# Retention and SwiGLU on one core: the chain of chunk states reads its pairs from PSUM

## The chip, the cores and the metric

The kernel runs on one core of a Trainium2 chip. The metric is the time of one execution on the device in microseconds. The engines work on their own instruction streams and are ordered by semaphores: TensorE (PE in the profile) multiplies matrices into PSUM, VectorE (DVE), ScalarE (ACT) and GpSimd (POOL) do elementwise work, and SyncE (SP) issues transfers.

## The reference

Two blocks follow each other. The first is a retention layer without softmax, on 8 batches, 8 heads, 576 positions and 64 values per head:

```python
scores = scale * np.matmul(q, k.transpose(0, 1, 3, 2))
Dmat = np.where(rel >= 0, gamma[:, None, None] ** rel[None, :, :], 0.0)   # rel = row - column
ret = scores * Dmat[None, :, :, :]
return np.matmul(ret, v)
```

Its output, with the heads laid side by side, is a matrix of 4608 tokens by 512. The second block is a SwiGLU feed-forward layer on it:

```python
g = x @ w_gate                       # 512 -> 1536
silu = g * (1.0 / (1.0 + np.exp(-g)))
return (silu * (x @ w_val)) @ w_out  # 1536 -> 512
```

All of it is fp32.

## The kernel before

**Retention.** Since the decay is a power of the distance, a head's 576 positions are cut into 9 chunks of 64. Within a chunk the scores are computed, masked with the decay and multiplied by v. What earlier chunks contribute comes through a state of 64 x 64 values for each chunk, which is the last state times a decay plus the chunk's own product of keys and values. Two heads are worked on at once, one on each half of the 128 partitions. That makes 4 head pairs per batch (`HP`) and 32 in all, numbered `i` from 0.

The products of keys and values of 8 chunks are made by `new_states` (L542) in `z`, which is half of a PSUM tile of two banks called `inner`: `z[:, 0]` has the even chunks, in one bank, and `z[:, 1]` the odd ones, in the other, 4 chunks of 64 columns each. The other halves of the two banks hold the scores, `sc` (L572). From `z` the states are made in four steps, in the function `masked`:

- `copies` (L583): ScalarE copies `z[:, 0]` to `even` in SBUF.
- `pairs` (L593): VectorE makes, for each pair of chunks, decay x `even` + `z[:, 1]`, and writes the 4 results into the odd places of `state` in SBUF.
- `odd` (L598): three VectorE instructions of 64 columns run along the chain of pairs: each is two chunks' decay times the last odd state plus the pair's own value, in place.
- `evens` (L603): one VectorE instruction makes the other states out of the odd ones and `even`.

Beside them, `own` (L579) masks the scores and `last` (L588) those of the ninth chunk. `earlier_values` (L558) multiplies the finished states with the queries in PSUM's tile `outer`, one tick later, and `to_x` writes the result into the feed-forward input.

**Feed-forward.** The first 512 tokens are done plainly: `up0` (L761, L766) and `down0` (L773). The other 4096 go in four tiles of 1024 tokens, with a fast scheme of 26 products per 4 x 4 x 4 block product: `up_step` (L992) and `down_step` (L1039) each multiply one combination of operands into one of four PSUM banks, `bankA` to `bankE`, in turn; `reads` (L926, L929, L1013, L1016, L1019) has ScalarE, VectorE and GpSimd combine the banks' contents with partial sums in SBUF. The sums of operands (`add`, L795, and L963) are made by VectorE and GpSimd as they come up.

**Order.** The order on each engine is the order in which the kernel is written out (a manual schedule). A `tick(t)` sends TensorE the products of head pair `t-1` and the values of `t-2`; what VectorE and ScalarE have to do for them is cut in pieces. The first four pairs, `i < HP`, are done at the start. Pairs 4 to 11 come while the first tokens pass `up0` and `down0`, with all pieces at once. From pair 12 on the ticks are spread among the steps of the first and later tiles, and `part_on` and `go_on` put one piece, or one part of one, behind the next step; `pairs`, `odd` and `evens` are three such parts. Before the next tick sends TensorE its products, all remaining pieces are written out.

Each engine takes its instructions strictly in order, so a bank read (L929) that stands behind a part of the state update waits for it, and so does the next matmul into that bank. `z` is one buffer: the next pair's `new_states` waits until it has been read.

Of the kernel before, what the change touches and what calls it, by code (L numbers as in the profile page):

```python
# [17 lines left out]
ALU = mybir.AluOpType  # L18
# [136 lines left out]
def kernel(  # L155
# [32 lines left out]
    nc = tc.nc  # L188
# [5 lines left out]
    HP = H // 2  # L194
    L = D
    NC = S // L
    NFULL = S // P
# [29 lines left out]
    z = inner[:, :, 256:512].rearrange("p r (c d) -> p r c d", d=D)  # L227
# [21 lines left out]
    at = [4096 + 512 * i for i in range(4)] + [x0_at + 512 * i for i in range(4)]  # L249
# [84 lines left out]
    step = tab[:, 2 * H : 2 * H + 2 * HP]  # L334
# [96 lines left out]
    even = const.tile([P, NFULL, D], F32, name="even")  # L431
# [8 lines left out]
    def places(i):  # L440
        return other if i < HP and i % 2 else (ret, ret_last, state)

    def last_scores(i):
        return bankE[:, 0:L] if i < HP else sr
# [10 lines left out]
    def vector(i):  # L455

        return i == 0
# [117 lines left out]
    def masked(i):  # L575
        p, sr, (ret, ret_last, state) = i % HP, last_scores(i), places(i)

        def own():
            nc.vector.tensor_tensor(out=ret, in0=sc, in1=near[:, 2 * p : 2 * p + 2].unsqueeze(2).to_broadcast([P, 2, NFULL, L]),  # L579
                                    op=ALU.mult)  # L580

        def copies():
            (nc.vector.tensor_copy if vector(i + 1) else nc.scalar.copy)(out=even, in_=z[:, 0])  # L583

        odd_states = state[:, 1:].rearrange("p (c r) d -> p c r d", r=2)[:, :, 1]

        def last():
            nc.vector.tensor_tensor(out=ret_last, in0=sr, in1=last_near[:, p], op=ALU.mult)  # L588

        def pairs():  # L590

            at = odd_states
            nc.vector.scalar_tensor_tensor(out=at, in0=even, scalar=step[:, p : p + 1], in1=z[:, 1], op0=ALU.mult, op1=ALU.add)  # L593

        def odd():
            at = odd_states
            for c in range(1, NFULL):
                nc.vector.scalar_tensor_tensor(out=at[:, c], in0=at[:, c - 1], scalar=step[:, HP + p : HP + p + 1],  # L598
                                               in1=at[:, c], op0=ALU.mult, op1=ALU.add)

        def evens():
            at = state[:, 0 : NC - 1].rearrange("p (c r) d -> p c r d", r=2)
            nc.vector.scalar_tensor_tensor(out=at[:, :, 1], in0=at[:, :, 0], scalar=step[:, p : p + 1], in1=even,  # L603
                                           op0=ALU.mult, op1=ALU.add)

        return [copies, own, [last, pairs, odd, evens]]

    def to_x(i):
# [66 lines left out]
    def tick(t, lo=HP, hi=NP, spread=False, then=None):  # L675
        go_on(len(pieces))
        if hi == HP:

            if lo <= t - 1 < hi:
                scores(t - 1, True)  # L680
                new_states(t - 1)
                pieces.extend(masked(t - 1))
                go_on(3)
            if lo <= t - 2 < hi:
                own_values(t - 2)
            for f in transposes(t) if lo <= t < hi else ():
                f()
            if t + 1 == HP:
                split(0)
            if lo <= t - 2 < hi:  # L690
                earlier_values(t - 2)
                if t == HP:
                    rounding(2)
                    rounding(3)
                to_x(t - 2)[0]()
            if t + 1 == HP:
                rounding(0)
            return
# [8 lines left out]
        if lo <= t - 1 < hi and whole(t - 2) and not whole(t - 1):  # L707
            decay(slice(0, H), slice(0, H), half[1])
        copies, *masks = masked(t - 1) if lo <= t - 1 < hi else (lambda: None,)
        keys, *new = transposes(t) if lo <= t < hi else (lambda: None,)  # L710
        outputs = to_x(t - 2)[0] if lo <= t - 2 < hi else lambda: None
# [96 lines left out]
    for line in OUT_SUMS:  # L808
        i, s = line.split("|")
# [395 lines left out]
```

## Time and profile before

| | us |
|---|---|
| median of three runs | 1046.8 |
| lowest and highest run | 1046.59 and 1056.34 |
| the profiled execution's own time | 1047.18 |
| its span, first to last instruction | 1045.5 |
| TensorE busy | 1027.6 |
| VectorE busy | 653.9 |
| GpSimd busy | 401.9 |
| ScalarE busy | 297.2 |

In lines of the profile, `128x64 f32<-128x64 f32 x90` means 128 partitions of 64 elements written and read, 90 instructions. Behind the bar of a group stand its busy time in us and the mean of one in ns, then the engine's idle time just before them with what ended it. A line of the timeline has start and duration in us. `x3` there is three instructions in a row, shown as one. TensorE's granted clock is at full speed (0.998).

### The profile page before, as it was taken

The numbers are of one execution on the slowest core, as the hardware profiler recorded it, in microseconds if no ns is written. First come the engines' busy times: TensorE is split into PE (matmuls) and PEld (weight loads), VectorE is DVE, ScalarE is ACT, GpSimd is POOL, SyncE is SP. The second block draws the span as 40 slices with busy tenths as digits, with TensorE's granted clock in tenths as the row PEclk, the third lists the DMA queues.
The fourth block names the chain that finished last, engine by engine and source line by source line (L and its number), as shares of the span: only waits on it lengthen the run. The fifth ranks groups of instructions, "written<-read, shape, count | busy, mean of one in ns | idle before, by whom it ended". The sixth has DMA issues, their size and how long they took to land.

```text
span 1045.5 us, 21496 instructions
## 1 busy us (share of the span) xinstructions
PE 1027.6 (98%) x8448; PEld 843.9 (81%) x8448; DVE 653.9 (63%) x1063; ACT 297.2 (28%) x646; POOL 401.9 (38%) x347
## 2 busy tenths in 40 slices
PE   7999999999999999999999999999999999999998
PEld 6444555888888888888888888888888888888887
DVE  4678878777769757555357786535476644344644
ACT  3466423243533222232322102223120022231110
POOL 2002367767476035612223048312250483222505
PEclk9999999999999999999999999999999999999999
DMA  9999867776678887665676777545554565555653
GB/s 248 242 283 258 198 197 267 207 212 182 186 204 227 239 249 200 193 178 149 176 220 159 214 182 220 154 136 155 154 174 140 153 200 152 152 153 161 181 161 101
DMA packets 310380, 199.10 MB, mean 190 GB/s; under 512 B 220168, under 2 KB 254984, under 8 KB 310280
## 3 DMA queue, kind: packets, MB, share of 16 engines
q1 hardware_dynamic: 279000, 161.51, 57.2%
q10 hardware_dynamic: 31280, 36.22, 10.4%
q8 instruction: 67, 1.10, 0.5%
q14 instruction: 33, 0.27, 0.1%
HBM read 157.56 MB, written 40.11 MB: 189 GB/s over the span
## 4 chain that ended last, share of the span: by engine, by line
PE 76%; DVE 4%; DMA 1%; ACT 0%; issue 0%; POOL 0%; ACTq 0%; DVEq 0%
PE bankC L992 12%; PE bankE L992 12%; PE bankA L992 11%; PE bankB L992 11%; PE bankA L1039 6%; PE bankB L1039 6%; PE bankC L1039 6%; PE bankE L1039 6%; DVE rest L929 1%; PE outer L531 1%; PE inner L572 1%; DVE state L598 1%; PE outer L558 1%; PE inner L542 1%; DVE arena L1016 1%
## 5 line engine op out<-in xcount | busy, mean ns | idle before, releaser
L929 POOL TENSOR_TENSOR rest<-rest 128x512 f32<-128x512 f32 x65 | 92.1, 1421 | 296.7 <-DVE rest L929 277.9
L1013 ACT ACTIVATE io<-rest 128x256 f32<-128x256 f32 x180 | 74.9, 416 | 305.3 <-DVE rest L929 259.1
L992 PE MATMUL bankA<-rest,arena 128*128 128x256 f32 x544 | 128.9, 380 | 1.8 <-DVE rest L929 1.0
L992 PE MATMUL bankC<-rest,arena 128*128 128x256 f32 x544 | 129.2, 380 | 1.4 <-DVE rest L929 1.4
L795 POOL TENSOR_TENSOR arena<-arena 128x512 f32<-128x512 f32 (+1 forms) x72 | 112.5, 1574 | 38.3 <-DMA up<-arena 22.4
L992 PE MATMUL bankE<-rest,arena 128*128 128x256 f32 x512 | 121.4, 380 | 1.0 <-DVE rest L929 1.0
L992 PE MATMUL bankB<-rest,arena 128*128 128x256 f32 x512 | 121.2, 379 | 0.0
L992 PEld LDWEIGHTS bankA<-rest,arena 128*128 128x128 f32 x544 | 103.0, 190 | 16.9 <-issue 1.9
L1020 POOL TENSOR_TENSOR arena<-rest,io 128x256 f32<-128x256 f32 x72 | 52.1, 729 | 167.3 <-ACT io L1013 167.3
L992 PEld LDWEIGHTS bankC<-rest,arena 128*128 128x128 f32 x544 | 102.8, 190 | 16.3 <-issue 1.8
L992 PEld LDWEIGHTS bankE<-rest,arena 128*128 128x128 f32 x512 | 97.0, 190 | 14.7 <-DVE rest L929 1.4
L992 PEld LDWEIGHTS bankB<-rest,arena 128*128 128x128 f32 x512 | 97.0, 190 | 13.4 <-issue 0.2
L795 POOL TENSOR_TENSOR rest<-rest 128x256 f32<-128x256 f32 (+1 forms) x66 | 67.8, 1048 | 100.9 <-DVE rest L419 61.2
L929 DVE TENSOR_TENSOR rest<-bankB,rest 128x512 f32<-128x512 f32 x72 | 48.8, 686 | 65.6 <-PE bankB L992 49.7
L929 DVE TENSOR_TENSOR rest<-bankC,rest 128x512 f32<-128x512 f32 x72 | 48.9, 687 | 64.6 <-PE bankC L992 45.9
L929 DVE TENSOR_TENSOR rest<-bankA,rest 128x512 f32<-128x512 f32 x72 | 48.8, 685 | 61.1 <-PE bankA L992 43.5
L929 DVE TENSOR_TENSOR rest<-bankE,rest 128x512 f32<-128x512 f32 x71 | 48.2, 687 | 60.5 <-PE bankE L992 46.1
L1016 DVE SCALAR_TENSOR_TENSOR arena<-rest,io 128x256 f32<-128x256 f32 x84 | 57.8, 689 | 11.1 <-ACT io L1013 10.9
L1039 PE MATMUL bankC<-arena 128*128 128x256 f32 x252 | 58.4, 381 | 0.3 <-issue 0.3
L1039 PE MATMUL bankB<-arena 128*128 128x256 f32 x252 | 58.3, 381 | 0.0
L1039 PE MATMUL bankA<-arena 128*128 128x256 f32 x252 | 58.0, 380 | 0.2 <-DVE arena L795 0.2
L1039 PE MATMUL bankE<-arena 128*128 128x256 f32 x252 | 57.9, 379 | 0.0
(189 smaller groups left out, 1632.4 us busy)
## 6 DMA issues: line engine op xcount, KB each, us to landing
arena<-up SPq DMA_DIRECT2D x234, 256.0 KB, 2.7
arena<-dn SPq DMA_DIRECT2D x104, 384.0 KB, 3.9
up<-arena ACTq DMA_DIRECT2D x78, 256.0 KB, 4.1
dn<-rest SPq DMA_DIRECT2D x78, 128.0 KB, 1.9
out_dram<-rest SPq DMA_DIRECT2D x31, 256.0 KB, 3.7
qk<-in_q_dram SPq DMA_DIRECT2D x108, 72.0 KB, 2.4
qk<-in_k_dram SPq DMA_DIRECT2D x108, 72.0 KB, 3.1
rest<-in_moe_w_out_dram ACTq DMA_DIRECT2D x6, 1024.0 KB, 5.4
```

The costliest lines, as they stand in the source:

```text
L531: m = nc.tensor.matmul(value(i, hl, c), s["v"][rows, at], ret[rows, c % 2 if whole(i) else hl, c // 2], start=start, stop=start, skip_grou ...
L542: nc.tensor.matmul(z[half[hl], r, c], s["kn"][chunk(i, hl, 2 * c + r, i < HP)], s["v"][rows, at], start=True, stop=True, skip_group_check= ...
L558: nc.tensor.matmul(xr[half[hl]] if c + 1 == NC else value(i, hl, c), state[half[hl], c, :], s["qT"][half[hl], column(i, hl, c)], start=Fal ...
L572: nc.tensor.matmul(sc[chunk(i, hl, 2 * c + r)[0], r if whole(i) else hl, c], kT[half[hl], at], qT[half[hl], at], start=True, stop=True, sk ...
L598: nc.vector.scalar_tensor_tensor(out=at[:, c], in0=at[:, c - 1], scalar=step[:, HP + p : HP + p + 1], in1=at[:, c], op0=ALU.mult, op1=ALU.add)
L795: eng.tensor_tensor(out=dst, in0=srcs[0], in1=srcs[1], op=ALU.add if op[0] == "add" else ALU.subtract)
L929: eng.tensor_tensor(out=at(op[1]), in0=at(op[2]), in1=at(op[3]), op=ALU.add if op[0] == "add" else ALU.subtract)
L992: m = nc.tensor.matmul(b[:, gv * TB : (gv + 1) * TB], w[:, gv, ts(c, P)], rhs[:, c, :], start=(opens and gv == 0 and c == 0), stop=(c == 1 ...
L1013: nc.scalar.activation(out=s, in_=src[:, 0:TB], func=AF.Silu, scale=-1.0 if negative else 1.0)
L1016: return lambda: nc.vector.scalar_tensor_tensor(out=dst, in0=src[:, TB : 2 * TB], scalar=-1.0, in1=s, op0=ALU.mult, op1=ALU.mult)
L1020: nc.gpsimd.tensor_tensor(out=dst, in0=src[:, TB : 2 * TB], in1=s, op=ALU.mult)
L1039: nc.tensor.matmul(b[:, m * TB : (m + 1) * TB], lhs[:, qd, ts(m, P)], w[:, qd], start=(opens and qd == 0 and m == 0), stop=(qd == NQ - 1), ...
```

## The change

For pairs from 4 on (`i >= HP`), only the first of the four pair states is written to `state`. The other three are written back to the place in `z[:, 1]` that they were read from, in PSUM. The chain, `odd`, then takes its second input from there, and `evens` takes the even chunks' products from `z[:, 0]` in place of the copy `even`. The copy is still made, since `pairs` reads it. For the first four pairs all is as before.

```diff
         odd_states = state[:, 1:].rearrange("p (c r) d -> p c r d", r=2)[:, :, 1]
+        firsts, summed = (NFULL, odd_states) if i < HP else (1, z[:, 1])
...
         def pairs():

-            at = odd_states
-            nc.vector.scalar_tensor_tensor(out=at, in0=even, scalar=step[:, p : p + 1], in1=z[:, 1], op0=ALU.mult, op1=ALU.add)
+            for at, c in ((odd_states[:, :firsts], slice(0, firsts)), (summed[:, firsts:], slice(firsts, NFULL))):
+                if firsts < NFULL or c.start == 0:
+                    nc.vector.scalar_tensor_tensor(out=at, in0=even[:, c], scalar=step[:, p : p + 1], in1=z[:, 1, c],
+                                                   op0=ALU.mult, op1=ALU.add)

         def odd():
             at = odd_states
             for c in range(1, NFULL):
                 nc.vector.scalar_tensor_tensor(out=at[:, c], in0=at[:, c - 1], scalar=step[:, HP + p : HP + p + 1],
-                                               in1=at[:, c], op0=ALU.mult, op1=ALU.add)
+                                               in1=summed[:, c], op0=ALU.mult, op1=ALU.add)

         def evens():
             at = state[:, 0 : NC - 1].rearrange("p (c r) d -> p c r d", r=2)
-            nc.vector.scalar_tensor_tensor(out=at[:, :, 1], in0=at[:, :, 0], scalar=step[:, p : p + 1], in1=even,
+            nc.vector.scalar_tensor_tensor(out=at[:, :, 1], in0=at[:, :, 0], scalar=step[:, p : p + 1], in1=even if i < HP else z[:, 0],
                                            op0=ALU.mult, op1=ALU.add)
```

## The prediction

> **What bounds the kernel now.** I read the page first, then TensorE's gaps, then the VectorE rows the change touches, then the two places where they meet.
>
> ```profile
> span 1045.5 us, 21496 instructions
> PE 1027.6 (98%) x8448; PEld 843.9 (81%) x8448; DVE 653.9 (63%) x1063; ACT 297.2 (28%) x646; POOL 401.9 (38%) x347
> ```
>
> TensorE is busy for all but 17.9 us of the span. About 8 us of that lie at the start and the end. So no edit to VectorE can give more than what is left in TensorE's gaps, and the question is which gaps these instructions cause. The waits of TensorE, longest first, name them:
>
> ```profile
> PE bankA L471 <- DMA qk<-in_q_dram: 4.3, 1, 4.3
> PE bankC L476 <- issue: 1.7, 1, 1.7
> PE bankC L992 <- DVE rest L929: 1.4, 1, 1.4
> PE bankA L992 <- DVE rest L929: 1.0, 1, 1.0
> PE bankE L992 <- DVE rest L929: 1.0, 1, 1.0
> PE bankA L992 <- ACT rest L926: 0.7, 1, 0.7
> PE outer L566 <- DVE kT L489: 0.5, 1, 0.5
> ```
>
> The columns are: total us, times, longest. Three waits for a bank that VectorE has still to read out (L929) make 3.4 us. Next the groups of VectorE, shapes kept apart (busy us, mean ns):
>
> ```profile
> L598 DVE SCALAR_TENSOR_TENSOR state<-state,tab 128x64 f32<-128x64 f32 x90 | 43.3, 481 | 2.9
> L603 DVE SCALAR_TENSOR_TENSOR state<-state,tab,even 128x256 f32<-128x256 f32 x30 | 14.3, 477 | 0.0
> L593 DVE SCALAR_TENSOR_TENSOR state<-even,tab,inner 128x256 f32<-128x256 f32 x30 | 14.1, 471 | 0.0
> ...
> L588 DVE TENSOR_TENSOR ret_last<-outer,last_near 128x64 f32<-128x64 f32 x28 | 6.0, 214 | 0.0
> ```
>
> L598, the chain of states, has a mean of 481 ns, while the answer on that line gives 271/285/1853 ns as least, median and most. A quarter of the length of L593's operands can't cost more than L593 does: the excess over 285 ns is a stall inside the instruction. Summed over all 96 of them it is 17.7 us, and only 0.1 us of it lies in the first four head pairs, which the change leaves alone. L593, which takes one input from PSUM, never exceeds 472 ns. The timeline shows where a stalled L598 meets a gap of TensorE (start, duration; the bracket is idle time before):
>
> ```profile
> 318.45 0.68 DVE L929 TENSOR_TENSOR rest<-bankB,rest 128x512 f32<-128x512 f32 x1
> 319.05 3.29 DVE L598 SCALAR_TENSOR_TENSOR state<-state,tab 128x64 f32<-128x64 f32 x3
> 322.27 1.28 DVE L929 TENSOR_TENSOR rest<-bankC,rest 128x512 f32<-128x512 f32 x2
> ...
> 319.23 1.27 POOL L963 TENSOR_TENSOR arena<-arena 128x512 f32<-128x512 f32 x1
> 320.45 1.81 POOL L795 TENSOR_TENSOR arena<-arena 128x768 f32<-128x768 f32 x1
> ...
> 323.69 1.97 PE L992 MATMUL bankC<-rest,arena 128*128 128x256 f32 x8 [1.44 <-DVE rest L929]
> ```
>
> Three chain steps take 3.29 us instead of 0.93 (3 x 285 and two gaps of 36 ns), and end with the GpSimd instruction beside them, at 322.26. The bank reads queued behind them end at 323.5, and TensorE starts late by 1.44 us. The same at 265 to 269 us: three steps take 2.75 us beside GpSimd additions, two reads of bankA follow to 268.9, and bankA's next matmul has waited 1.04 us.
>
> **What the Trainium skill says.** "SBUF — State Buffer", section "Who interferes with whom": "A DVE instruction with two SBUF inputs contends with a GpSimd instruction that reads SBUF"; the later one waits for the whole of the other. The trace agrees: L598 has two SBUF inputs and reaches 1853 ns beside GpSimd, L593 with one stays at 472. "VectorE: DVE Perf Modes", section on the TRN2 errata, prices a PSUM source at 120 cycles plus the elements against 58 for SBUF at 0.96 GHz, so 65 ns more. The trace disagrees: 256 elements take 471 ns with a PSUM input (L593) and 479 without (L603). I keep 65 ns as an upper bound for the forms not shown here. "PSUM — Partial Sum Buffer", on bank collisions, says that software must keep two engines off one bank; so the bank of z stays closed to TensorE until VectorE's last read of it.
>
> **The change part by part.** It acts in 28 of the 32 head pairs.
>
> Pairs (L593). One instruction of 256 elements becomes two, 64 elements to SBUF and 192 to PSUM. The slope comes from two rows: 64 elements take 214 ns (L588), 512 take 691 (median of L579), so 1.065 ns per element. Then 64 cost 471 - 192 x 1.065 = 267 ns, and 192 cost 471 - 64 x 1.065 = 403 ns, plus a gap of 36: together 706 instead of 471. No row shows VectorE writing PSUM. Below, there is no reason that it beats an SBUF write by more than the 14 ns between L598's least and median; above, 65 ns. I take 0.
>
> Chain (L598). Three steps read one input from PSUM: 267 instead of 285 ns, and no second SBUF input, so the stalls go. Gain 54 ns, and the 17.6 us.
>
> Even states (L603). In1 comes from PSUM: 471 instead of 479 ns.
>
> Sum without stalls, from start to end of a head pair's states: now 1.83 us (471 + 3 x 285 + 479, three gaps of 36, an overlap of 83); after, 2.00. So VectorE does 0.17 us more, 4.8 us over 28, against 17.6 us of stalls: 12.8 us net of its 654. If each of the six PSUM forms cost 65 ns more, it is 0.56 us each, 15.7 us in all.
>
> What of it lies on the path. At 322 us: the reads of bankC would run at 320.2 to 321.4, TensorE is ready at 322.25; the gap of 1.44 goes, with 0.8 us to spare. At 268 us: the reads of bankA end at 267.3 and TensorE is ready at 268.0; 1.04 goes, with 0.7 to spare. The 0.51 us before L566 at 274.9 waits for the key transposition (L489), at the end of a run of VectorE and ScalarE work that started behind the same stall: ScalarE's two SiLUs, its scalings of k and q and then the transposes move up by about 1.6 us, TensorE by 1.04; 0.51 fits. Sum 2.99 us. The third wait (bankE, 1.0 us at 192.8) ends a VectorE-bound run from 164 us on; pair 11 (counted from 0) at that run's head carries only 0.11 us of stall, against 0.17 more work: plus 0.06.
>
> Where do the other stalls go? 17.6 minus those at the two places (1.8 and 2.4) were hidden: VectorE idles after them, waiting for TensorE. What is late next after 323 us is VectorE's sums for the down projection; VectorE moves up by 2.2 us there and TensorE by 1.44, so the 0.2 us wait at 361 doesn't grow.
>
> Added waits. The even states now read z, so TensorE's next new_states (L542) waits for them, and not for the pairs alone. Behind L542 stand that tick's matmuls and all feed-forward steps. From the end of L603 to the next L542 there are at least 3.19 us (near 120 to 139 us, and more later): 0.17, or 0.56, is covered. Before L558, which reads the states, the least is 0.76 us, at pair 11: 0.06 is covered there too. ScalarE's copy of z[:, 0] into `even` need wait only for the pairs: no gain, since it comes 5.4 us or more after L603. The pairs' second half waits for its first, counted. No DMA moves, and SP's queue stays as it is. A few instructions of ScalarE and one sum of GpSimd name a DMA semaphore that another wait had implied until now. ScalarE's are loads ordered two head pairs ahead; the GpSimd sum, at 329.6 us, waits 7.4 us for VectorE anyway. I cost them at nothing.
>
> **Sum.** 1047.18 - 2.99 + 0.06 = 1044.25 against the profiled execution's own time; the median of the runs is 0.38 below that: 1043.9 us.
>
> **The rivals.**
> - Hidden anyway, or the lock moves on. VectorE's next instruction with two SBUF inputs meets the GpSimd work that L598 met. For: L1016 (two SBUF inputs) shows 1.24 us beside GpSimd for a row of 0.42. Against: at both places the next in line reads a bank, with one SBUF input. If it comes behind the bank reads, the transposition's 0.51 and one of the two gaps (1.44) stay: 1043.9 + 1.95 = 1045.8; with all of it kept, 1046.8.
> - Slower. The longer state update delays the bank reads queued behind it where no stall is removed. It pays per head pair what TensorE can't wait: 0.17 us, 0.56 with the skill's price. It decides where a bank read has less slack than that. Now TensorE waits for L929 in three places only, so few can be that close; were all 28 exposed at 0.17, it costs 4.8 and the sum is 1043.9 + 4.8 = 1048.7; at 0.56, 1059.6. Slower than before needs 18 exposed pairs at 0.17, or 6 at 0.56.
> - The change does not do what it says: PSUM operands don't spare the lock. L593's 472 ns at most speaks against it. It would end at 1046.8 plus part of the 0.17s, 1047.5.
>
> **How the numbers follow.** Forecast 1043.9 (1043 to 1045): 0.52. Lock moves or hidden (1045 to 1047.2): 0.28. No sparing: 0.05. Slower (from 1047.2, mostly to 1049): 0.11. Another 0.04 for a gain over 4 us, if GpSimd runs freer as well. Leaving out what is above 1047.5 and below 1042.8 gives the range. A difference of 1% is 10.5 us, about what a measurement of this kernel can tell from no change; only slower at the skill's price with nearly all pairs exposed reaches it (0.04), and no gain does, as TensorE's gaps hold too little (0.01).
>
> **What would show it.** L598's mean falls to about 270 ns with no long ones, its input named inner; L593 splits into some 267 and 403; VectorE's busy time falls to about 641 us, or stays above 648 where the lock moves on to L1016 or L1019; TensorE's waits for L929 on bankC (1.4) and bankA (1.0) are gone. I would be wrong if the 192-element form took far over 470 ns, if L542 waited for VectorE, or if new waits for L929 appeared at other ticks.

## The result, and the profile after

The changed kernel takes 1043.78 us (median of 20 runs), against 1047.6 for the kernel before (20 runs). The ratio is 0.9959, with a 95% interval of 0.9944 to 0.9973: between 2.8 and 5.9 us off, or 4.3. The profiled execution has a time of its own of 1045.08 us, 2.1 below that of before. Single runs of one kernel lie up to 4.4 us below their median and up to 8.7 above it, so one time tells little here, and the experiments go by intervals and by where TensorE waits. (The two medians lie 3.8 us apart; the ratio is the better guide.)

Line numbers move by up to three: L593 has become L595, L598 is L601, L603 is L606, L929 is L932, L992 is L995 and L1039 is L1042. The page of after:

```profile
span 1043.4 us, 21528 instructions
...
PE 1026.9 (98%) x8448; PEld 842.8 (81%) x8448; DVE 641.2 (61%) x1091; ACT 296.8 (28%) x646; POOL 400.4 (38%) x347
```

VectorE lost 12.7 us of busy time with 28 instructions more. Its groups for the states, shapes kept apart (busy us, mean ns):

```profile
L601 DVE SCALAR_TENSOR_TENSOR state<-state,tab,inner 128x64 f32<-128x64 f32 x84 | 23.5, 280 | 2.7
L606 DVE SCALAR_TENSOR_TENSOR state<-state,tab,inner 128x256 f32<-128x256 f32 x28 | 13.3, 474 | 0.0
L595 DVE SCALAR_TENSOR_TENSOR inner<-even,tab,inner 128x192 f32<-128x192 f32 x28 | 11.8, 423 | 1.0
L595 DVE SCALAR_TENSOR_TENSOR state<-even,tab,inner 128x64 f32<-128x64 f32 x28 | 7.6, 270 | 0.0
```

The answer on the chain's line has the spread (least, median and most of one, ns):

```profile
L601 DVE SCALAR_TENSOR_TENSOR state<-state,tab,inner x84: 267/281/283, 63.9 to 774.4; 128x64 f32<-128x64 f32 x84
```

No step of the changed pairs is longer than 283 ns; before, the most was 1853. The timeline at head pair 16, where TensorE lost 1.44 us before:

```profile
317.47 0.90 DVE L601 SCALAR_TENSOR_TENSOR state<-state,tab,inner 128x64 f32<-128x64 f32 x3
318.29 1.28 DVE L932 TENSOR_TENSOR rest<-bankC,rest 128x512 f32<-128x512 f32 x2
...
317.41 1.27 POOL L966 TENSOR_TENSOR arena<-arena 128x512 f32<-128x512 f32 x1
318.64 1.82 POOL L798 TENSOR_TENSOR arena<-arena 128x768 f32<-128x768 f32 x1
...
318.53 1.89 PE L995 MATMUL bankB<-x_odd,arena 128*128 128x256 f32 x8
320.26 1.89 PE L995 MATMUL bankC<-rest,arena 128*128 128x256 f32 x8
```

GpSimd does the same two instructions in the same time, but the three chain steps pass beside the first of them in 0.90 us in place of 3.29. The bank is read out by 319.57, and TensorE takes it up at 320.26 without a wait. TensorE's waits in the profile of after, longest first:

```profile
PE bankA L471 <- POOL near L343: 4.3, 1, 4.3
PE outer L531 <- DVE arena L418: 2.1, 1, 2.1
PE bankC L1042 <- issue: 1.0, 1, 1.0
PE bankB L471 <- DMA kn<-in_k_dram: 0.7, 1, 0.7
PE bankA L995 <- ACT rest L929: 0.6, 1, 0.6
```

The waits for L929 of before (1.4, 1.0 and 1.0 us) and the one for the key transposition (0.5) are gone, but for 0.1 us. In this execution TensorE loses more in the start (L531 2.1 us, 0.4 before) and inside the down projection (1.0, 0.3 before). The stretch from the first L992 (L995) to the first L1039 (L1042), in which the first tile of 1024 tokens passes `up_step`, takes 146.71 us (177.00 to 323.71) in place of 151.14 (176.08 to 327.22). About 0.9 us of these 4.4 is the wait at 192.8 us, which is no gain (see below). What comes after, up to the end of the last matmul, takes 715.84 in place of 714.42. (The 26 products of the fast scheme are for a block product of 4 x 2 x 4, in the down projection 4 x 4 x 2, and not 4 x 4 x 4.)

### The profile page after: what moved, and what is told of

It is laid out like the page before. It is cut to its first block, busy times and chain, and to the rows that moved or that the text cites. A ratio compares the mean times of both kernels' runs of the same rounds, so it can differ in the third digit from the quotient of the medians.

```text
span 1043.4 us, 21528 instructions
## 1 busy us (share of the span) xinstructions
PE 1026.9 (98%) x8448; PEld 842.8 (81%) x8448; DVE 641.2 (61%) x1091; ACT 296.8 (28%) x646; POOL 400.4 (38%) x347
## 4 chain that ended last, share of the span: by engine, by line
PE 68%; DVE 2%; issue 1%; DMA 1%; ACT 1%; SPq 1%; POOL 0%; ACTq 0%; DVEq 0%
PE bankE L995 11%; PE bankC L995 11%; PE bankB L995 10%; PE bankA L995 10%; PE bankB L1042 6%; PE bankC L1042 6%; PE bankA L1042 6%; PE bankE L1042 5%; PE outer L531 1%; PE outer L558 1%; PE inner L572 1%; PE inner L542 1%; DMA up<-arena 1%; SPq L293 0%; DVE rest L932 0%
## 5 line engine op out<-in xcount | busy, mean ns | idle before, releaser
L932 POOL TENSOR_TENSOR rest<-rest 128x512 f32<-128x512 f32 x65 | 91.6, 1414 | 300.5 <-DVE rest L932 278.7
L1016 ACT ACTIVATE io<-rest 128x256 f32<-128x256 f32 x180 | 74.8, 416 | 305.6 <-DVE rest L932 261.6
L995 PE MATMUL bankA<-rest,arena 128*128 128x256 f32 x544 | 128.8, 380 | 0.6 <-ACT rest L929 0.6
L995 PE MATMUL bankC<-rest,arena 128*128 128x256 f32 x544 | 129.0, 380 | 0.0
L995 PE MATMUL bankE<-rest,arena 128*128 128x256 f32 x512 | 121.4, 380 | 0.1
L995 PE MATMUL bankB<-rest,arena 128*128 128x256 f32 x512 | 121.2, 379 | 0.0
L995 PEld LDWEIGHTS bankA<-rest,arena 128*128 128x128 f32 x544 | 103.1, 190 | 15.5 <-ACT rest L929 1.0
L995 PEld LDWEIGHTS bankC<-rest,arena 128*128 128x128 f32 x544 | 102.9, 190 | 14.4 <-POOL arena L798 0.3
L995 PEld LDWEIGHTS bankE<-rest,arena 128*128 128x128 f32 x512 | 97.0, 190 | 13.7 <-DVE rest L932 0.5
L995 PEld LDWEIGHTS bankB<-rest,arena 128*128 128x128 f32 x512 | 97.1, 190 | 13.3
L932 DVE TENSOR_TENSOR rest<-bankB,rest 128x512 f32<-128x512 f32 x72 | 48.9, 687 | 67.8 <-PE bankB L995 51.8
L932 DVE TENSOR_TENSOR rest<-bankC,rest 128x512 f32<-128x512 f32 x72 | 48.9, 687 | 65.1 <-PE bankC L995 46.2
L932 DVE TENSOR_TENSOR rest<-bankA,rest 128x512 f32<-128x512 f32 x72 | 48.9, 687 | 63.8 <-PE bankA L995 46.4
L932 DVE TENSOR_TENSOR rest<-bankE,rest 128x512 f32<-128x512 f32 x71 | 48.2, 687 | 61.2 <-PE bankE L995 46.7
L1019 DVE SCALAR_TENSOR_TENSOR arena<-rest,io 128x256 f32<-128x256 f32 x84 | 55.7, 664 | 11.3 <-ACT io L1016 11.1
L1042 PE MATMUL bankC<-arena 128*128 128x256 f32 x252 | 58.4, 381 | 1.5 <-issue 1.0
L1042 PE MATMUL bankB<-arena 128*128 128x256 f32 x252 | 58.3, 381 | 0.3 <-DVE arena L798 0.3
L1042 PE MATMUL bankA<-arena 128*128 128x256 f32 x252 | 58.0, 380 | 0.2 <-DVE arena L798 0.2
L1042 PE MATMUL bankE<-arena 128*128 128x256 f32 x252 | 57.9, 379 | 0.0
```

The lines of the kernel that those rows point to most:

```text
L932: eng.tensor_tensor(out=at(op[1]), in0=at(op[2]), in1=at(op[3]), op=ALU.add if op[0] == "add" else ALU.subtract)
L995: m = nc.tensor.matmul(b[:, gv * TB : (gv + 1) * TB], w[:, gv, ts(c, P)], rhs[:, c, :], start=(opens and gv == 0 and c == 0), stop=(c == 1 ...
L1016: nc.scalar.activation(out=s, in_=src[:, 0:TB], func=AF.Silu, scale=-1.0 if negative else 1.0)
L1019: return lambda: nc.vector.scalar_tensor_tensor(out=dst, in0=src[:, TB : 2 * TB], scalar=-1.0, in1=s, op0=ALU.mult, op1=ALU.mult)
L1042: nc.tensor.matmul(b[:, m * TB : (m + 1) * TB], lhs[:, qd, ts(m, P)], w[:, qd], start=(opens and qd == 0 and m == 0), stop=(qd == NQ - 1), ...
```

## The experiments

The first theory is the prediction's: the chain's second SBUF input makes it wait for GpSimd, and this reaches TensorE at pairs 13 and 16 alone. The main rival was that stalls cost a little at all pairs. Each ratio compares a kernel with the kernel before on the same chip; the latter's median was 1050.4, 1047.5 and 1049.6 us on the three chips used, so the text goes by ratios. A "stretch" below is that of the first tile, from one execution each.

### One part alone

In the first kernel `evens` reads the copy `even` as before; the rest is as in the changed kernel, against which the edit is shown.

```diff
-            ... in1=even if i < HP else z[:, 0],
+            ... in1=even,
```

> The pairs and the chain as in the changed kernel, the even states from the copy in SBUF as before. Theory (the second SBUF input of the three chain steps is what stalls, and only at head pairs 13 and 16 does it reach TensorE): the chain steps stay at 281 ns, no wait of TensorE for L932 over 0.2 us near 268 and 320 us, time as the changed kernel, about 3 us under the one before. Rival (the even states' read of PSUM brings a part): at least 1 us of the gain is missing, and L606 shows stalls over 100 ns.

Measured: ratio 0.9953 (0.9931 to 0.9974), 4.9 us off. No chain step of the changed pairs stalls, the stretch is 147.87 us, and the waits at 268, 275 and 322 us are gone. TensorE waits 0.6 us for a bank near 193 us, where VectorE comes from the operand sums.

The second has only the even states changed:

```diff
-            ... scalar=step[:, p : p + 1], in1=even,
+            ... scalar=step[:, p : p + 1], in1=even if i < HP else z[:, 0],
```

> Only the even states read PSUM; pairs and chain as before. Theory: L603 takes 475 ns in place of 479, the chain still stalls by about 17 us in all, the waits of 1.4 and 1.0 us are there, time within 1 us of the kernel before. Rival (the even states bring a part, or letting go of z later costs something): time moves by more than 1.5 us either way.

Measured: ratio 0.9996 (0.9977 to 1.0014). The even states take 473 ns, the chain stalls by 19.0 us in all, the stretch is 151.64 us, and the waits are there:

```profile
PE bankC L992 <- DVE rest L929: 2.1, 1, 2.1
...
PE bankA L992 <- DVE rest L929: 0.9, 1, 0.9
PE outer L566 <- DVE kT L489: 0.5, 1, 0.5
```

So the gain belongs to the chain. The part of the even states can't be told from nothing (2.4 us off to 1.5 over).

### What the added instruction costs without what it spares

The pairs are split in 64 and 192 elements, but both go to `state`, and all later steps read SBUF.

```diff
-        firsts, summed = (NFULL, odd_states) if i < HP else (1, z[:, 1])
+        firsts, summed = (NFULL if i < HP else 1, odd_states)
...
-            ... in1=even if i < HP else z[:, 0],
+            ... in1=even,
```

> The pairs split in two instructions (64 and 192 elements) as in the change, but both written to SBUF, and the chain and the even states read SBUF as before: the change's added instruction without what it spares. Theory: 0.2 us more of VectorE per pair, the 192 elements take 403 to 423 ns, the stalls and TensorE's waits at 268 and 322 us stay or grow by up to 0.2 us each; time 0 to 1 us over the kernel before. Rival (a longer update costs per pair): 4 to 5 us over.

Measured: ratio 0.9998 (0.9983 to 1.0014), so nothing that can be seen (1.8 us off to 1.5 over). The 192 elements take 408 ns to SBUF, against 423 to PSUM in the changed kernel: the write to PSUM costs 15 ns. The stalls stay (18.1 us), the stretch is 152.16 us, and the wait at pair 16 grew from 1.4 to 2.1 us, by more than the 0.2 expected. The split is not needed for that: with the even states alone changed it was 2.1 us as well.

### Which pairs

The condition `i < HP` is replaced by one on the pair, in `firsts, summed` and in `evens`. First the two pairs with a gap behind them, and all the others:

```diff
-        firsts, summed = (NFULL, odd_states) if i < HP else (1, z[:, 1])
+        firsts, summed = (1, z[:, 1]) if i in (13, 16) else (NFULL, odd_states)
```

> The change in head pairs 13 and 16 alone. Theory (all the other stalls are hidden): VectorE loses only 4 us of its 17 us of stalls, yet the waits near 268, 275 and 322 us are gone, and the time is that of the changed kernel within 1 us, 2.5 to 3.5 us under the one before. Rival (the 17 us of stalls slow TensorE a little everywhere): about a quarter of the gain, 0.5 to 1 us.

Measured: ratio 0.9989 (0.9972 to 1.0007): 1.2 us off, with an interval from 2.9 off to 0.7 over. In its profile the chain still stalls by 17.1 us, the three waits at 268, 275 and 322 us are gone, and the stretch is 147.89 us.

> The change in the 26 head pairs other than 13 and 16. Theory: VectorE loses 13 us of stalls, but the waits of TensorE for L932 near 268 and 322 us stay (1.0 and 1.4 us, and 0.5 us for the key transposition), and the time is within 1 us of the kernel before. Rival (stalls cost everywhere): three quarters of the gain, 2 to 3 us.

Measured: ratio 0.9985 (0.9971 to 0.9998), 1.6 us off (0.2 to 3.0). The chain stalls only at pairs 13 and 16 (1.8 and 2.4 us), the waits are there (1.4, 0.9 and 0.5 us), and the stretch is 150.44 us. The profiles agree with the first theory. The times fit it less well: their middles have some of the gain missing in the one, and some of it present in the other, though both intervals still reach what was expected (2.5 us off in the first, under 1 in the second). The stalls hint at a reason. Those of pairs 13 and 16 are the same in each profile that has them (1.8 and 2.4 us), but pair 12 stalls by 3.0 us in the profile before and not in that of the even states alone, and pair 15 by 0 and 2.8 us. The meetings with GpSimd differ between executions. This led to a second theory: it is the stretch that counts, whichever of its pairs is hit. Pairs 12 to 16 against all others:

```diff
+        firsts, summed = (1, z[:, 1]) if 12 <= i <= 16 else (NFULL, odd_states)
```

> The change in head pairs 12 to 16 alone, those whose states are made while the first tile of 1024 tokens passes up_step, about 170 to 325 us. Theory (stalls count where TensorE uses a bank again within 1 us of VectorE's read of it, which is this stretch, on whichever pair the stall falls in an execution): the stretch from the first L995 to the first L1042 takes 146.5 to 148 us, as in the changed kernel, against 151.1 before, and the time is 3 to 4 us under the kernel before. Rival (the gain is spread over all pairs): 5 of 28 pairs, under 1 us.

Measured: ratio 0.9957 (0.9939 to 0.9974), 4.5 us off (2.7 to 6.4), as much as the whole change brings. The stretch is 148.03 us; 10.1 us of stalls remain elsewhere.

> The change in head pairs 4 to 11 and 17 to 31, not in 12 to 16. Theory: the stretch from the first L995 to the first L1042 stays at 150.5 to 152 us, everything after it within 1 us of the kernel before, and the time is within 1 us of it. Rival (the gain is spread over all pairs): 2.5 to 3.5 us under the kernel before.

Measured: ratio 0.9997 (0.9984 to 1.001), 0.3 us off (1.7 off to 1.0 over), nothing that can be seen. The stretch is 151.19 us. In its profile VectorE is rid of 13 us of stalls, and TensorE waits as before:

```profile
PE bankC L995 <- DVE rest L932: 1.5, 1, 1.5
PE bankE L995 <- DVE rest L932: 1.0, 1, 1.0
PE bankA L995 <- DVE rest L932: 0.9, 1, 0.9
...
PE outer L566 <- DVE kT L489: 0.5, 1, 0.5
```

Then the pairs of the stretch taken apart:

> The change in head pairs 12, 14 and 15 alone, the rest of those of the first tile. Theory (13 and 16 carry the gain): the waits near 268, 275 and 322 us stay, time within 1 us of the kernel before. Rival (the stalls at 12, 14 and 15, which differ from execution to execution, reach TensorE in some of them): 1.5 to 3 us under the kernel before.

Measured: ratio 0.9984 (0.997 to 0.9998), 1.7 us off (0.2 to 3.1). The stretch in its profile is 151.02 us, as before the change, with the waits of 0.9, 0.5 and 1.4 us in it.

> The change in head pairs 13 and 16 alone, a second time, beside 12, 14 and 15 on the same chip, since the first run's interval reached from 2.9 us under the kernel before to 0.7 over it. Theory: 2.5 to 4 us under the kernel before. Rival: 1 to 2 us, with the remainder at 12, 14 and 15.

Measured: ratio 0.9976 (0.9958 to 0.9994), 2.5 us off (0.6 to 4.4). The stretch in its profile is 149.37 us, without the three waits. By their middles the two add up to 4.2, near the 4.5 of the five pairs, but the intervals are too wide to say how the gain is shared.

The profiles speak for 13 and 16. In the six in which these two read SBUF beside all of GpSimd's sums the stretch takes 150.4 to 152.2 us; in the other eight it takes 146.7 to 149.4. They also show one way in which 14 and 15 count. In the two of those six in which 14 and 15 stall as well (the even states alone, and the split in SBUF) TensorE's wait at pair 16 is 2.05 and 2.13 us; in the other four, where they don't, it is 1.44 or 1.45. With the even states alone changed, pair 16 looks so:

```profile
319.86 3.29 DVE L598 SCALAR_TENSOR_TENSOR state<-state,tab 128x64 f32<-128x64 f32 x3
...
321.26 1.80 POOL L795 TENSOR_TENSOR arena<-arena 128x768 f32<-128x768 f32 x1
...
320.55 1.89 PE L992 MATMUL bankB<-x_odd,arena 128*128 128x256 f32 x8
324.49 1.97 PE L992 MATMUL bankC<-rest,arena 128*128 128x256 f32 x8 [2.05 <-DVE rest L929]
```

Beside the profile of before, GpSimd's last sum starts and the chain ends 0.8 us later, while TensorE's last step in front of the wait starts only 0.2 us later (320.36 there). This fits stalls of 14 and 15 that delay GpSimd and reach TensorE where pair 16 stalls too, by 0.6 to 0.7 us. That 12, 14 and 15 are worth the 1.7 us of their run is not shown.

### How much the bank reads have to spare

The first instruction of the pairs, 64 elements to `state`, is issued two or five more times in pairs 4 to 31.

```diff
+            parts = [(odd_states[:, :firsts], slice(0, firsts)), (summed[:, firsts:], slice(firsts, NFULL))]
-            for at, c in ((odd_states[:, :firsts], slice(0, firsts)), (summed[:, firsts:], slice(firsts, NFULL))):
+            for at, c in parts[:1] * (2 if firsts < NFULL else 0) + parts:
```

> The changed kernel with the first instruction of the pairs (64 elements, 270 ns) issued three times in place of once in pairs 4 to 31, so 0.6 us more of VectorE per pair in front of the chain. Theory (0.7 us to spare at the bank reads behind the chain at pairs 13 and 16, more elsewhere): no new wait of TensorE over 0.2 us, time within 1 us of the changed kernel. Rival (bank reads everywhere stand close, a longer state update costs per pair): 0.6 us for most of 28 pairs, 10 to 17 us more.

Measured: ratio to the kernel before 0.9969 (0.9958 to 0.998), while the changed kernel has 0.9959 (0.9944 to 0.9973). By the middles about 1 us of the gain is spent, but the intervals overlap. No wait behind the chain at 268 or 322 us came back. The 0.5 us for the key transposition did, and near 188 to 195 us, where VectorE makes operand sums, there are 0.6, 0.3 and 0.5 us, so the expectation that no new wait would pass 0.2 us did not hold.

> The same with six in place of one, 1.5 us more of VectorE per pair, which is what the chain's stalls cost at their worst. Theory: waits of TensorE for L935 come back at pairs 13 and 16 with about 0.8 us each, and perhaps 0.5 us for the key transposition; pairs outside 12 to 16 cost nothing; time 1.5 to 3 us above the changed kernel, near the kernel before. Rival: 1.5 us for most of 28 pairs, 25 to 42 us more.

Measured: ratio 1.0032 (1.002 to 1.0045), 3.4 us over the kernel before and 7 to 8 over the changed one, more than expected. (The 1.5 us are less than the worst stalls, which took 1.8 to 3.0 us. Lines stand one further down in this kernel; the L935 expected is its L933.) Among TensorE's waits:

```profile
PE inner L542 <- issue: 2.4, 2, 1.6
...
PE bankB L1043 <- DVE arena L799: 1.8, 1, 1.8
PE bankB L996 <- DVE rest L933: 1.0, 2, 0.5
PE bankE L777 <- DVE arena L770: 0.8, 1, 0.8
```

At pair 13 it waits 0.62 us (0.50 and 0.12 for two banks) and at pair 16 0.67 us (0.55 and 0.12), near the 0.8 expected. The rest lies elsewhere, and the largest part is the wait of `new_states`:

```profile
144.53 0.48 DVE L607 SCALAR_TENSOR_TENSOR state<-state,tab,inner 128x256 f32<-128x256 f32 x1
...
145.11 0.69 PE L542 MATMUL inner<-v,kn 64*64 64x64 f32 x32 [1.58 <-issue]
```

The profile names no releaser, but L542 starts 0.10 us after VectorE's last read of `z` has ended, and the one at 133.97 starts 0.11 us after 133.86. This fits the added wait of the change: `pairs`, the last reader before it, ends some 1.3 us earlier in both places (143.66 and 132.52).

### The kernel before, with less GpSimd work beside it

```diff
-            if i > 1:
+            if i > 1 and qd == 0:
                 w_sums(qd, i)
```

> The kernel before, without GpSimd's sums of gate and value weights (L795 and L963 in w_sums) in the second and third of the three column blocks of the first tile: part of the computation is left out, and TensorE multiplies unsummed weights in their place. Theory (GpSimd's reads are what the chain's second SBUF input waits for): with no GpSimd work beside them, the chain steps of head pairs 12, 13 and 15 take 285 ns and no more, those of 16 too but for what the down projection's first sum still overlaps, and the waits of 1.0 and 1.4 us shrink or go. Rival (the stall comes from something else, such as the loads running then): the steps of pairs 13 and 16 still take 1.2 us and more.

Measured: the chain steps of pairs 12 to 15 don't stall, those of 16 by 0.84 us, and the stretch takes 147.57 us with no wait at 268, 275 or 322 us. One time was taken, 1045.26 us. At pair 13, with GpSimd idle from 266.0 on, and at pair 16, with one instruction beside it:

```profile
267.19 0.91 DVE L598 SCALAR_TENSOR_TENSOR state<-state,tab 128x64 f32<-128x64 f32 x3
...
319.20 1.76 DVE L598 SCALAR_TENSOR_TENSOR state<-state,tab 128x64 f32<-128x64 f32 x3
...
318.42 1.82 POOL L795 TENSOR_TENSOR arena<-arena 128x768 f32<-128x768 f32 x1 [1.57 <-PE bankB L992]
```

The chain is that of the kernel before, with both inputs in SBUF. Here it stalls only where a GpSimd instruction runs, and until about that one's end (320.24). The profile of before says the same of all its stalls: each of the 27 chain steps that take over 300 ns overlaps a GpSimd instruction, and 24 of them end 0.08 us after one has ended. (Not every overlap stalls: 11 steps that overlap one take 300 ns or less.)

## Why the prediction was right, point by point

**The cause.** "The excess over 285 ns is a stall inside the instruction", of an instruction with two SBUF inputs beside GpSimd. Shown from both sides: with the input in PSUM the stall goes though GpSimd runs on (the timeline of after), and with GpSimd's sums left out it goes though the input stays in SBUF (one profile). The price of a PSUM source in the Trainium skill, "VectorE: DVE Perf Modes", section on the TRN2 errata, 65 ns over SBUF, does not hold for these forms: with one of two inputs in PSUM, 64 elements take 270 to 281 ns, and 285 with both in SBUF. What "SBUF — State Buffer", section "Who interferes with whom", says of two SBUF inputs beside a GpSimd read agrees with these runs: 27 of the 27 stalled steps of before lie beside GpSimd.

**The durations.** 267 and 403 ns were said for the split pairs; 270 and 423 were measured. 15 of the 20 ns are the write to PSUM, which I had taken at 0, with 65 as the upper end. A chain step has a median of 281, not 267, and the even states 474, not 471. From start to end a pair's states take 2.07 us in place of the 2.00 predicted, so 0.24 more than before and not 0.17. VectorE's busy time was put at 641 us, and is 641.2, but that it fits so closely is in part luck: the lines of the states lost 11.9 us and not 12.8, and the other lines some 0.9 in all, where L1016 (L1019) alone lost 2.1 and others gained.

**Which waits go.** The 1.44 at 322 us, the 1.04 at 268 us and the 0.51 of the key transposition went, as said; the lock did not move on to L1016. The third, 1.0 us at 192.8 us, was to stay at plus 0.06, and shrank to 0.10. That is no gain: in both kernels TensorE starts this matmul when VectorE has read the bank, at 192.84 and 192.80 us; after, TensorE came there later, since it lost more in the start. In these two executions the bank read makes up for what TensorE gained or lost before that point.

**The size.** 2.99 us was the sum; the ratio gives 4.3 (2.8 to 5.9), so the sum lies inside the interval, near its lower end. If it was too small, the step is "Where do the other stalls go? 17.6 minus those at the two places (1.8 and 2.4) were hidden". For the stalls of pairs 4 to 11 and 17 to 31 no loss is seen: changed alone they bring 0.3 us (1.0 over to 1.7 off). For pairs 12, 14 and 15 it is doubtful: they bring 1.7 (0.2 to 3.1), and in the profiles in which 14 and 15 stall the wait at pair 16 is 0.6 to 0.7 us longer. They are in the same stretch, and in the one execution that the prediction read only pair 12 of them stalls, by 3.0 us and hidden. That the median came out at 1043.78, so close to 1043.9, is luck in part: the prediction started from a median of before of 1046.8, which is 1047.6 over 20 runs.

**The added waits.** Not met in the changed kernel: L542 waits 0.2 us for ScalarE and 0.4 for GpSimd, and no wait of it names VectorE. But "at least 3.19 us" is less room than it seems. It should have covered 1.5 us more per pair, and did not. The likely reason, not tried by itself, is that VectorE has next to no idle time around pairs 7 to 9 (one wait of 1.6 us from 124 to 145 us in that profile), so that the delays of successive pairs add up. The slower rival named the bank reads as its mechanism; when the update was made longer still, `new_states` and VectorE's sums cost more than the bank reads did. No run here tests the rule on banks that the prediction cites: `new_states` overwrites what VectorE reads there, and has to wait for that in any case.

## What to carry to other kernels

When an instruction's mean is far above its median, read the most of it and look at what runs beside the long ones: the stall beside GpSimd's SBUF reads was taken away here by moving one input to PSUM, at some 0.2 us per use. What it brings is only what TensorE waited behind it: here five of 28 uses brought as much as all of them. And one profile shows one meeting of two engines; where stalls differ between executions, as they do here at pairs 12, 14 and 15, read several profiles before counting a stall as hidden.

## What I had not expected

- A VectorE write to PSUM costs 15 ns more than one to SBUF (423 and 408 ns for 192 elements with the same inputs).
- The same kernel's stalls differ between executions at some places (pair 12: 3.0 or 0 us, pair 15: 0 or 2.8 us) and are equal to 0.1 us at others (pairs 13 and 16, 1.8 and 2.4 us in each profile that kept the SBUF input there and GpSimd's sums).
- `earlier_values` (L558) waits near 165 us for the even states of pair 11 in seven of the profiles, by 0.5 to 1.7 us, where the profile before had 0.76 us to spare. In six of them the chain of pair 11 is unchanged, in the seventh (all pairs outside 12 to 16) it is changed. That one brought no time that can be seen, so the wait may not count in the end; its cause stays open.
